# Eight first-layer groups of a block in seven products, and a sum over halves of tokens moved to two DMAs

## The chip, the cores and the metric

The kernel runs on one core of a Trainium2 chip. The metric is the device time of one execution in microseconds (us); lower is better. The core has engines that run side by side, each through its own list of instructions in order: TensorE (PE) multiplies matrices into PSUM, VectorE (DVE), ScalarE (ACT) and GpSimd (POOL) work elementwise, and SyncE (SP) issues DMAs. DMAs move data on 16 DMA engines; those issued by SP go through a hardware queue (q1 in the profile), those issued by POOL through a software queue (q0).

## The reference

Attention with keys and values projected to 64 rows, then a two-layer network with a hard-swish between the layers, over 8 batches of 1024 tokens:

```python
k_proj = np.einsum('ks,bhsd->bhkd', E, k)
v_proj = np.einsum('ks,bhsd->bhkd', F, v)
scores = scale * np.matmul(q, k_proj.transpose(0, 1, 3, 2))
attn = np.exp(scores - np.max(scores, axis=-1, keepdims=True))
attn = attn / (np.sum(attn, axis=-1, keepdims=True) + 1e-09)
x = np.matmul(attn, v_proj)          # to 8192 tokens of 512
h = x @ w_in                          # 512 to 2048
g = h * np.clip(h + 3.0, 0.0, 6.0) / 6.0
out = g @ w_out                       # 2048 to 512
```

## The kernel before, in words

**Blocks.** Each batch b is two blocks (t = 0 and 1) of 512 tokens. The main loop (line 858) runs over batches 1 to 7; batch 0 is worked ahead of it. In a block PE computes the first layer of this block, `h` in 16 groups of 128 columns, and the second layer of the block behind it. Attention of the next batch (`second`) and the projection of the one after that (`third`) are fitted in at places that a plan names.

**The order is written out.** A string names the steps of a block one by one (`ORDER`, and `QUADS` from batch 3 on), and every engine gets its instructions in that order. `L0` to `L15` are first-layer groups: 8 matmuls of 512 columns into a PSUM tile `mm` (`first_group`, line 581), then `h_out` (573): ACT writes relu(h/6 + 0.5) to `r`, DVE writes min(r, 1) times h to `g`. The PSUM pools hold four tiles `mm` and four tiles `at`.

**The second layer in pairs.** `A`, `B` and `N` steps are the seven products of Strassen's scheme (in Winograd's form) for the second layer; A and B belong to the block behind, N starts on this block. Each is 16 matmuls of 256 columns (`Pair`, 684). They need sums of blocks of `g`, made by class `Sums` (662): `c` adds the first half of tokens of the eight low groups to the second half, into a tile `sc` (on POOL); `a` changes the second half in place to a difference (DVE); `b` and `d` make `sb` (DVE) and `sd` (POOL). Step 5 reads `sc`, step 6 the result of `a`, steps 1 and 3 `sb` and `sd`.

**The first layer in a quad.** From batch 3 on the last four groups of a block (12 to 15) are also made in seven products, steps `Q1` to `Q7` of 8 matmuls of 256 columns each (`Quad`, 746), from four sums of x (`xc`, `xa`, `xb`, `xd`, POOL) and three sums of w_in (`v_sums`, made in batch 1; two blocks of w_in are changed in place in batch 3). ACT copies products 7, 2 and 5 out of PSUM (`copied`, 773), DVE subtracts, and `out` (778) applies the hard-swish: three of four outputs by ACT (relu), POOL (min with 1, line 789) and POOL (product, 790), the fourth by ACT and DVE.

**Delays.** `behind_steps(n)` lets an instruction be recorded n steps later; `later` holds small works that are taken one at a time after certain steps.

**Queues.** SP's queue holds, in this order within a batch, stores of output rows (709), the inverse sums and their spreading (330, 336), and the transposes of keys and queries (251, 188). POOL's queue issues the loads of k, v and q of a later batch (`load_kqv`, 124), each set behind a one-element copy `mark` (218) that waits for the transposed queries. The plan of batch 3 issues such a load at the start of its first block; from then on `third.load_next` issues it at `L7` of a second block.

The order from batch 3 on before the change:

```python
    QUADS = ("L0 A7 L1 A6 L2 B7 L3 A1 L4 B2 L5 A3 L6 B5 L7 A4 "
             "L8 Q7 Q2 B6 L9 Q6 N2 Q5 B1 L10 Q1 B3 L11 Q3 N5 B4 Q4").split()
```

## Time and profile before

| what | value |
|---|---|
| time, median of 3 runs | 478.25 us (477.89 to 478.27) |
| the profiled execution's span | 476.3 us |
| PE / PEld busy | 99% / 73% |
| DVE / ACT / POOL busy | 71% / 58% / 64% |
| DMA packets, bytes moved | 84609, 68.65 MB |
| output stores (SP), median to landing | 4.2 us for 256 KB |
| spread sums (SP), median to landing | 6.1 us for 256 KB |
| loads of k, v, q (POOL), 1 MB each, median to landing | 11.4, 15.9, 21.0 us |
| granted TensorE clock | 1.00 in every window asked for |

The span is the time from the first to the last instruction of the profiled execution; the measured time has about 2 us more around it. In a line of the trace's groups, such as `L790 POOL TENSOR_TENSOR g<-r,qm 128x512 bf16<-128x512 f32 x27 | 36.3, 1345 | 2.3`, the fields are the source line, engine, operation, written and read tiles, shapes, how many, then total busy us and mean ns of one, then the idle time of the engine just ahead of them. In a timeline the first number is the start in us from the span's start and the second the length. Lengths of matmuls overlap, so what a step costs is read from start to start.

### The profile page before, as it was taken

How to read it: one execution, taken by the hardware profiler on the slowest of the kernel's cores; microseconds unless marked ns; L12 is line 12 of the kernel's file. 1: busy time of each engine (PE TensorE's matmuls, PEld its weight loads, DVE VectorE, ACT ScalarE, POOL GpSimd, SP SyncE). 2: the span in 40 equal slices, each digit the busy share in tenths (PEclk: the TensorE clock that was granted, in tenths of full speed). 3: DMA queues.
4: the chain of work that ended last, by engine and by line, in shares of the span. 5: the costliest groups of instructions: out<-in, count | busy, mean ns of one | idle time of the engine just before them, and what ended most of it. 6: DMA issues, size and time to landing. Idle time of an engine off the chain costs nothing.

```text
span 476.3 us, 14916 instructions
## 1 busy us (share of the span) xinstructions
PE 469.6 (99%) x6428; PEld 346.1 (73%) x6428; DVE 339.4 (71%) x542; ACT 275.4 (58%) x534; POOL 306.1 (64%) x207
## 2 busy tenths in 40 slices
PE   7999999999999999999999999999999999999997
PEld 4554567667677766787787878778687877878797
DVE  2583387688765958886778876887778897747574
ACT  3766478675455654656466565666457545546451
POOL 8634966153335232867897778887788587888820
DMA  9999989688999939996999196962931054111012
GB/s 166 198 200 207 240 146 207 124 144 149 238 180 156 214 100 200 200 206 157 192 165 171 48 228 136 211 126 89 205 101 47 36 125 136 45 47 45 33 59 90
DMA packets 84609, 68.65 MB, mean 144 GB/s; under 512 B 38336, under 2 KB 70592, under 8 KB 84544
## 3 DMA queue, kind: packets, MB, share of 16 engines
q0 software_dynamic: 33024, 29.36, 39.7%
q1 hardware_dynamic: 51152, 37.83, 33.1%
q8 instruction: 50, 0.82, 0.7%
q10 hardware_dynamic: 368, 0.52, 0.3%
q14 instruction: 15, 0.12, 0.1%
HBM read 71.83 MB, written 16.97 MB: 186 GB/s over the span
## 4 chain that ended last, share of the span: by engine, by line
PE 92%; DMA 3%; ACT 2%; POOL 1%; DVE 0%; issue 0%; POOLq 0%
PE mm L200 68%; PE at L200 21%; DMA w_in_sb<-in_moe_w_in_dram 2%; PE at L289 2%; DMA k<-in_k_dram 1%; PE at L268 1%; ACT aT L277 1%; POOL k L110 0%; POOL q L106 0%; PE at L459 0%; DVE parts L309 0%; ACT rec L212 0%; ACT rec L206 0%; ACT m L705 0%; PE at L439 0%
## 5 line engine op out<-in xcount | busy, mean ns | idle before, releaser
L200 PE MATMUL mm<-xT,w_in_sb 128*64 128x512 bf16 (+1 forms) x1808 | 221.8, 375 | 0.2
L576 DVE SCALAR_TENSOR_TENSOR g<-r,mm 128x512 bf16<-128x512 f32 x216 | 146.2, 681 | 70.7 <-ACT r L575 69.8
L575 ACT ACTIVATE r<-mm 128x512 f32<-128x512 f32 x216 | 128.3, 598 | 117.3 <-PE mm L200 111.1
L200 PEld LDWEIGHTS <-w_in_sb 128*64 128x64 bf16 x2048 | 117.0, 110 | 59.7 <-issue 3.3
L200 PEld LDWEIGHTS <-g 128*64 128x64 bf16 x2048 | 112.6, 110 | 24.0 <-issue 4.1
L139 POOL TENSOR_TENSOR sd<-g,sb 128x1024 bf16<-128x1024 bf16 x28 | 59.1, 2130 | 42.0 <-DVE sb L139 40.7
L136 POOL TENSOR_TENSOR sc<-g 128x2048 bf16<-128x2048 bf16 x14 | 57.0, 4072 | 44.7 <-DVE g L576 44.7
L200 PE MATMUL mm<-w_out_sb,g 128*64 128x256 bf16 (+1 forms) x1088 | 77.8, 286 | 0.0
L200 PE MATMUL at<-w_sums,g 128*64 128x256 bf16 x896 | 58.4, 273 | 0.3 <-DVE g L576 0.3
L789 POOL TENSOR_SCALAR r<-r 128x512 f32<-128x512 f32 x27 | 41.5, 1538 | 15.2 <-ACT r L784 15.2
L705 ACT COPY m<-at 128x256 f32<-128x256 f32 x84 | 31.4, 373 | 30.1 <-PE at L200 25.6
L790 POOL TENSOR_TENSOR g<-r,qm 128x512 bf16<-128x512 f32 x27 | 36.3, 1345 | 2.3
L301 DVE TENSOR_TENSOR xT<-at,rec 128x512 bf16<-128x512 f32 x54 | 34.9, 683 | 2.3 <-DMA rec<-turned_rows 1.6
L139 DVE TENSOR_TENSOR o_sb<-m,mm 128x256 f32<-128x256 f32 x60 | 24.8, 413 | 9.6 <-PE mm L200 7.3
L200 PE MATMUL mm<-w_out_sb,sd 128*64 128x256 bf16 x480 | 31.3, 273 | 0.0
L200 PE MATMUL mm<-w_sums,sb 128*64 128x256 bf16 x480 | 31.2, 273 | 0.0
L277 ACT ACTIVATE aT<-at 128x512 bf16<-128x512 f32 x52 | 29.6, 601 | 2.3 <-PE at L268 2.3
L309 DVE TRANSPOSE_TENSOR_REDUCE parts<-aT 128x32 f32<-128x1024 bf16 x24 | 29.7, 1236 | 0.3 <-ACT aT L277 0.3
L200 PEld LDWEIGHTS <-sd 128*64 128x64 bf16 x480 | 26.5, 110 | 3.9 <-issue 0.2
L200 PE MATMUL at<-w_out_sb,sc 128*64 128x256 bf16 x448 | 29.3, 273 | 0.0
L200 PEld LDWEIGHTS <-sc 128*64 128x64 bf16 x480 | 26.5, 110 | 3.8 <-issue 0.3
L200 PEld LDWEIGHTS <-sb 128*64 128x64 bf16 x480 | 26.2, 110 | 4.0 <-issue 1.6
(118 smaller groups left out, 496.3 us busy)
## 6 DMA issues: line engine op xcount, KB each, us to landing
out_dram<-o_sb SPq DMA_DIRECT2D x60, 256.0 KB, 4.2
rec<-turned_rows SPq DMA_DIRECT2D x48, 256.0 KB, 6.1
k<-in_k_dram POOLq DMA_DIRECT2D x7, 1024.0 KB, 11.4
v<-in_v_dram POOLq DMA_DIRECT2D x7, 1024.0 KB, 15.9
q<-in_q_dram POOLq DMA_DIRECT2D x7, 1024.0 KB, 21.0
w_in_sb<-in_moe_w_in_dram POOLq DMA_DIRECT2D x7, 256.0 KB, 9.9
w_out_sb<-in_moe_w_out_dram POOLq DMA_DIRECT2D x3, 512.0 KB, 14.2
k<-in_k_dram POOLq DMA_DIRECT2D x4, 256.0 KB, 6.0
```

The costliest lines, as they stand in the source:

```text
L136: engine.tensor_tensor(out=out, in0=x, in1=y, op=ALU.add)
L139: engine.tensor_tensor(out=out, in0=x, in1=y, op=ALU.subtract)
L200: nc.tensor.matmul(ps[lo:lo + width], stationary[:, lo:lo + width], moving, **flags)
L277: when(lambda r=r: nc.scalar.activation(aT[:, :, r, :], tiles[r].rearrange("p (a n) -> p a n", a=2), AF.Exp, scale=scale))
L289: nc.tensor.matmul(tiles[t][c:c + D], stationary(r, 2 * j + a), self.weights(j, a)[r:r + KP], start=True, stop=True)
L301: when(lambda t=t: nc.vector.tensor_mul(self.xT[:, j, t, :], av[t], rec[:, t]))
L309: nc.vector.tensor_reduce(out=self.parts[:, j], op=ALU.add, axis=mybir.AxisListType.X, apply_transpose=True, in_=self.aT[j].rearrange("p a ...
L575: nc.scalar.activation(r, h_ps, AF.Relu, bias=0.5, scale=1.0 / 6.0)
L576: when(lambda: nc.vector.scalar_tensor_tensor(g[:, fo, :], r, 1.0, h_ps, op0=ALU.min, op1=ALU.mult))
L705: self.copy(m, ps)
L789: nc.gpsimd.tensor_scalar(out=r, in0=r, scalar1=1.0, scalar2=None, op0=ALU.min)
L790: nc.gpsimd.tensor_tensor(out=g, in0=r3, in1=h3, op=ALU.mult)
```

## The change

1. From batch 3 on groups 8 to 11 of a block are made like groups 12 to 15: a second quad `R` with its own sums of w_in. Both quads use the same four sums of x, and their copies share the buffers `qm7`, `qm2`, `qm5`. `L8` to `L11` are gone from the order, `R1` to `R7` are added.
2. The clip of the six outputs of a block that POOL multiplies moves to ACT: relu(0.5 - h/6) and then relu(1 - r) in place of relu(0.5 + h/6) on ACT and min on POOL. These outputs are those of both quads; in the last block all go by DVE as before.
3. From batch 3 on `c` is two DMAs: `+c` copies the first half of tokens of the eight low groups into `sc` (SP's queue), `+C` adds the second half to it (POOL's queue; it waits for the copy). `a` of the low groups then waits for `+C`.
4. The orders are new: `b`, `d`, the sums of x, `c` and `a` stand in them as `+` entries, and there are two orders for the last batch. The works of attention stand in tables (`PLANS`) with other places: the load in batch 3 moves from the start of the first block to `L3`, the later loads from `L7` to `Q1` of the second block, and batches 1 and 2 have changed places too. The sums of w_in for both quads are made in batch 1, the in-place changes in batch 3 at `L1` and `L3`.
5. One spare buffer of `aT` goes (five to four), and `ones` is smaller. The rest of the diff is assertions that what a product reads has been written.

```diff
+ORDER_OF_QUADS = ('L0 R7 A7 L1 +b +x L2 L3 L4 +d L5 L6 B2 A6 R2 R6 L7 R5 B7 B5 A1 +c R1 Q7 B6 A3 +C R3 Q6 B1 '
+                  'A4 Q2 B3 N2 Q5 Q1 N5 +a R4 Q3 B4 Q4')
+ORDER_OF_LAST = (('R7 L0 +b +x L1 R2 L2 A7 A6 L3 L4 +d L5 L6 B2 R6 L7 R5 B7 B5 +c A1 Q7 R1 B6 +C A3 R3 Q6 B1 '
+                  'A4 Q2 B3 N2 Q5 Q1 N5 +a R4 Q3 B4 Q4'),
+                 ('L0 R7 +x A7 +b L1 L2 R2 L3 L4 L5 L6 B2 R6 A6 L7 R5 +d A1 B7 B5 Q7 R1 +c B6 A3 R3 Q6 +C B1 '
+                  'A4 Q2 B3 N2 Q5 Q1 N5 +a R4 Q3 B4 Q4'))
+PLANS = {
...
+    3: ('0.L1:S01 0.Q2:u0 0.L5:S23,u1 0.B5:u2 0.A1:u3 0.Q2:T 0.N2:I 0.B4:p 1.Q1:m 1.L3:V01 1.B1:V23 '
+        '0.L3:l 0.L1:iR 0.L3:iQ'),
+    4: ('0.L1:S01 0.Q2:u0 0.L5:S23,u1 0.B5:u2 0.A1:u3 0.Q2:T 0.N2:I 0.B4:p 1.Q1:m 1.L3:V01 1.B1:V23'),
+}
+RELU_BEHIND = 2
+PRODUCT_BEHIND = 3
+L_BEHIND = 1
...
+    quarters = {"Q": Quarter(FO - 2 * NQ), "R": Quarter(FO - 4 * NQ)}
...
         def c(self, engine=nc.gpsimd):
             self.sc = spool.tile([P, KH, HT], bf16, tag="sc", name="sc")
-            add(self.sc, self.blocks[0], self.blocks[2], engine)
...
+            if engine is None:
+                nc.sync.dma_start(out=self.sc, in_=self.blocks[0])
+            else:
+                add(self.sc, self.blocks[0], self.blocks[2], engine)
+
+        def c_added(self):
+            assert not self.ready
+            nc.gpsimd.dma_start(out=self.sc, in_=self.blocks[2], accum_op=ALU.add)
...
-                nc.scalar.activation(r, h, AF.Relu, bias=0.5, scale=1.0 / 6.0)
...
-                    nc.gpsimd.tensor_scalar(out=r, in0=r, scalar1=1.0, scalar2=None, op0=ALU.min)
+                    nc.scalar.activation(r, h, AF.Relu, bias=0.5, scale=-1.0 / 6.0)
+                    nc.scalar.activation(r, r, AF.Relu, bias=1.0, scale=-1.0)
                     nc.gpsimd.tensor_tensor(out=g, in0=r3, in1=h3, op=ALU.mult)
...
-            at((0, "A6"), lambda: add(v12, v12, v22, nc.gpsimd), lambda: sub(v21, v21, v22, nc.gpsimd))
```

In a plan an entry such as `1.Q1:m` reads: in the second block, after step Q1, do m. The letters are: S scores, V values, u the sums of exps, T and I the turning and spreading of these sums, P the projection of the next batch, p that of the batch after it, l the load behind the next batch, m the load behind the batch after it, w the sums of w_in and i the changes in place. At a step named in the `+` entries: b, d, x (sums of x), c, C, a.

## The prediction

> **What bounds the kernel now.** I read the share of each engine first, then TensorE (PE) in order of time in one block of batch 5, then the groups of instructions with their shapes kept apart. From the page:

> ```profile
> PE 469.6 (99%) x6428; PEld 346.1 (73%) x6428; DVE 339.4 (71%) x542; ACT 275.4 (58%) x534; POOL 306.1 (64%) x207
> PE mm L200 68%; PE at L200 21%; DMA w_in_sb<-in_moe_w_in_dram 2%; PE at L289 2%; DMA k<-in_k_dram 1%; PE at L268 1%; ACT aT L277 1%; POOL k L110 0%; POOL q L106 0%; PE at L459 0%; DVE parts L309 0%; ACT rec L212 0%; ACT rec L206 0%; ACT m L705 0%; PE at L439 0%
> ```

> PE is busy for 99% of the span and 89% of the chain that ended last is products of line 200. Every other engine has idle time. The timeline of PE (start, length, work) shows whether "busy" also means "at its pitch":

> ```profile
> 319.02 1.03 PE L200 MATMUL mm<-xT,w_in_sb 128*64 128x512 bf16 x8
> 319.89 0.60 PE L200 MATMUL mm<-xa,w_in_sb 128*64 128x256 bf16 x8
> 320.32 1.04 PE L200 MATMUL at<-w_sums,g 128*64 128x256 bf16 x16
> 321.20 0.60 PE L200 MATMUL at<-xc,w_in_sb 128*64 128x256 bf16 x8
> 321.63 1.04 PE L200 MATMUL mm<-w_sums,sb 128*64 128x256 bf16 x16
> ```

> From start to start: a plain group L (8 matmuls of 512 columns) takes 0.87 us, a step of a pair (16 of 256) 0.87 to 0.88, a step of a quad (8 of 256) 0.43. So 512 columns cost 108 ns, 256 cost 54 ns, and steps follow without a gap. A block of batches 3 to 7 has 12 L, 14 pair steps and 7 quad steps: 26 x 0.867 + 7 x 0.433 = 25.6 us. The last block (436.8 to 462.5) takes 25.7, so PE runs at its pitch there, and only fewer columns, or a stall, can move the time. Projection, scores and values add 4.8 us a batch (55.9 us a batch).

> **The products: minus 4.3 us.** In ten blocks the groups L8 to L11 (32 matmuls of 512 columns, 3.47 us) become seven R steps (7 x 0.433 = 3.03 us): 0.434 us less a block, 4.3 in all. A block is then 25.14 us of PE.

> **The other engines, priced where there is room.** VectorE (DVE): four products of 0.68 us become three subtractions and one product of 0.69; nothing changes. ScalarE (ACT) and GpSimd (POOL):

> ```profile
> L784 ACT ACTIVATE r<-qm 128x512 f32<-128x512 f32 x30 | 19.0, 633 | 9.2 <-DVE qm L139 9.2
> L775 ACT COPY qm<-at 128x512 f32<-128x512 f32 x30 | 16.4, 586 | 0.0
> L789 POOL TENSOR_SCALAR r<-r 128x512 f32<-128x512 f32 x27 | 41.5, 1538 | 15.2 <-ACT r L784 15.2
> L790 POOL TENSOR_TENSOR g<-r,qm 128x512 bf16<-128x512 f32 x27 | 36.3, 1345 | 2.3
> L136 POOL TENSOR_TENSOR sc<-g 128x2048 bf16<-128x2048 bf16 x14 | 57.0, 4072 | 44.7 <-DVE g L576 44.7
> ```

> ACT gains three copies of 0.586 and six clips of 0.633 a block, 5.6 us; it was busy for about 17.5 us of a first block (t=0) and 16 of a second, so it comes to 23.1 of 27.6 and 21.6 of 26.2. POOL loses the sum (4.07) and three clips (1.54 each), gains three products (1.345) and one DMA issue (0.9): minus 3.7. Both are hidden behind PE; if ACT's cover were gone, the 5.6 us would show (a rival below). The new plans of batches 1 and 2 and the new orders can recover at most the few tenths that PE stands still there: I take minus 0.3, bounds minus 1 and plus 2 (six weight sums of 1.16 us now stand together on POOL, ahead of the d sums of 4.2 us).

> **The sum of halves: where it goes.** It leaves POOL for a copy on SP's queue, a wait, and an adding DMA on POOL's queue. No row shows either, so I bound them.

> ```profile
> q0 software_dynamic: 33024, 29.36, 39.7%
> q1 hardware_dynamic: 51152, 37.83, 33.1%
> q<-in_q_dram POOLq DMA_DIRECT2D x7, 1024.0 KB, 21.0
> DMA to landing us min/median/max: 2.0/2.0/2.7
> DMA to landing us min/median/max: 2.0/5.8/8.3
> DMA to landing us min/median/max: 21.2/21.2/21.2
> ```

> (The last three: output stores from 400 to 450 us, with no load running; stores from 295 to 320, beside a load of the next batch; the q load of 295.5.) A packet of q1 takes 0.331 x 16 x 476.3 / 51152 = 49 ns for 740 bytes, one of q0 92 ns for 889. Each DMA here has 1024 pieces of 512 bytes, 64 to an engine. By bytes that is 34 ns x 64 = 2.2 us at q1's rate and 53 ns x 64 = 3.4 us at q0's; by packets of q0 it is 5.9 us, the upper end. The copy is q1's kind: 2.2 us. The add reads SBUF like the copy, but reads twice and goes through q0: I take the middle of the two rates, 2.8 us, and keep 2.2 and 5.9 for the range. Around the data the packet records show 0.83 us from issue to first packet on SP and 1.7 on POOL (0.9 of it the issue), and 0.3 from last packet to semaphore. So copy 3.3 us, add 4.8 us. A DMA cannot take less than its data, so no end is below nothing.

> [...]

> **When the add can start.** Times from a block's first matmul. In an unloaded second block (batches 3 to 6) V01 has added 0.55 us: step R1 ends at 14.85. Its subtraction on DVE (0.69) is done at 15.6; ACT first copies Q7 (ends 15.3) until 15.9, then clips R1 twice (0.63 each) until 17.1; POOL's product of R1 (1.35) stands ahead of the add and ends at 18.4. The copy is queued on SP behind the store of A1 (ended 14.4, subtraction 0.4, issue 0.33): out at about 15.2, landed at 18.5. So the add is issued at 18.4 and lands at 23.2. Who needs it: step N5, at 22.1 + 1.1 (values) = 23.2. No stall, no slack. Behind the waiting add on POOL stand the products of R3 and Q6; ACT's copy of Q2 waits for R3's (they share a buffer), and step Q5 for that copy: 0.3 us of room. On DVE the difference a of the low groups now waits for the add, and behind it the last products; what needs these is L2 of the next block, 3 us later.

> Batch 6, t=0: scores add 0.95, R1 ends later, add issued at 18.8, lands 23.6, N5 at 23.05: 0.55. Batch 7: nothing inserted, N5 at 22.1, add issued at 18.2, lands 23.0: 0.9 in each of two blocks.

> **Beside a load.** The load of a batch's k, v, q (three of 1 MB) occupies q0 for 21 us. In batches 3 and 4 it now starts at Q1 of the second block, behind the add and two products on POOL: first issue at 23.2, q out 1.8 later, landed 21.2 after that, so 20.0 us into the next first block (batches 4 and 5). There the copy, out at 15.4, shares the engines (stores took 5.8 instead of 2.0 us) and lands at about 20.5; the add lands at 25.3 against N5 at 23.05: 2.25 us, twice.

> Batch 3, t=0, is the worst. Before, the load was issued as the block began:

> ```profile
> 189.00 0.18 POOL L218 COPY mark<-qT 1x1 bf16<-1x1 bf16 x1 [8.82 <-DMA qT<-q]
> 189.23 0.93 POOL L124 DMA_DIRECT2D k<-in_k_dram  x1
> 189.94 1.28 DVE L301 TENSOR_TENSOR xT<-at,rec 128x512 bf16<-128x512 f32 x2
> ```

> Now it stands on POOL behind two in-place weight sums and the four sums of x, and xa needs the last xT (done at 191.2): three sums of 1.2 us, mark, k issued at 195.0, q at 196.8, landed at 218.0, that is 28.7 us into a block that began at 189.35. Loads on q0 land one behind the other (k 11, v 16, q 21 us), so the add's packets come after q's: 31.5 at the earliest. N5 stands at 23.05: 8.45 us.

> **The sum.** 8.45 + 2 x 2.25 + 0.55 + 2 x 0.9 = 15.3 of stalls, less 4.3 and 0.3: plus 10.7. The execution's span of 476.3 with 1.95 around it is the median of the runs, 478.25; so 489. With the add's data at 2.2 us the stalls are 11.8 (485.4); at 5.9 they are 11.55 + 2 x 5.35 + 3.65 + 4 x 3.1 + 2 x 4.0 = 46.3 (520).

> **Rivals.** (1) Everything lands in time: the fast side. Place: N5 of every block; decides from an add that lands by 23 us in every block, batch 3 too, which needs the add's packets to pass the load's, or the load to be through by 19. For it: PE loses nothing else, and in most blocks I find 0 to 0.9 us short, within the error of my chain. Against: landing order of k, v, q. Time: 478.25 - 4.6 = 473.6. (2) The add is slow (q0's price by packets, or by elements): each block pays 2 to 5 us; 495 to 520. For it: packets on q0 are nearly twice as dear as on q1. (3) ACT becomes the bound in first blocks, where exps come on top: 84% busy in order, 1 us in each of five blocks, DMAs in time but for batch 3: 478.25 - 4.6 + 8.45 + 5 = 487; alone without batch 3's stall 478.7.

> **Chances.** A difference under 0.2% cannot be told from none. Forecast (batch 3 pays, others little; 480 to 494): 0.45. Everything in time: 0.27. Slow add: 0.19. ACT, and mixtures around no change: 0.09. Faster 0.28, same 0.04, slower 0.68. The forecast's own range is 481 to 494. The whole range runs from 473 (rival 1) to 505 (half of rival 2).

> **What would show it.** Batch 3, t=0: PE idle about 8 us ahead of the products that read sc, released by a DMA on q0, landing after that load's q. Batches 4 and 5, t=0: some 2 us there; other blocks under 1. R steps at 0.43 us. Wrong if the wait for sc is under 1 us in batch 3, if the add's packets cost over 60 ns, or if PE waits mostly for r or qm from ACT.

## The result: 551 us, 15% slower, and the profile after

| | before | after |
|---|---|---|
| time, median | 478.10 us (4 runs) | 550.98 us (4 runs) |
| ratio, 95% interval | | 1.152 (1.150 to 1.155) |
| span of the profiled execution | 476.3 us | 548.3 us |
| mean granted TensorE clock | 1.00 | 0.947 |

The forecast, 489 (473 to 505), had the sign and the place of the loss right and its size far too small; it had the late landing, but no term for the clock. One execution each of e7, e9b and e14 (below) fell into a slow state, of 806 to 1236 us, and is left out of their ratios. The chain that ended last, before:

```profile
PE 92%; DMA 3%; ACT 2%; POOL 1%; DVE 0%; issue 0%; POOLq 0%
```

Five lines from the page of after: busy times, the granted clock in 40 slices, the chain that ended last, and the two new DMAs with their median from issue to landing.

```profile
PE 491.1 (90%) x6668; PEld 369.8 (67%) x6668; DVE 346.9 (63%) x545; ACT 319.7 (58%) x618; POOL 286.8 (52%) x212
...
PEclk9999999999999998599897998989989799798989
...
PE 61%; DMA 24%; POOL 4%; DVE 3%; ACT 3%; issue 3%; SPq 0%; POOLq 0%; DVEq 0%; ACTq 0%
...
sc<-g SPq DMA_DIRECT2D x10, 512.0 KB, 3.6
sc<-g POOLq DMA_DIRECT2D x10, 512.0 KB, 7.6
```

PE falls from 99% to 90% busy, the DMAs' share of the chain rises from 3% to 24%, the copy lands as forecast (3.6 us against 3.3) and the add does not (7.6 against 4.8). From the 16th slice on, within batch 3, the clock is no longer full. What PE waited for (total us, times, longest):

```profile
PEld L251 <- DMA sc<-g: 31.7, 10, 4.2
...
ACT qm L855 <- POOL g L877: 24.0, 10, 10.7
PE at L251 <- ACT qm L855: 19.9, 9, 10.5
```

Ten blocks, ten waits for the add. The other two lines are one chain: ACT may copy quad product 2 only when POOL has multiplied out of that buffer; POOL's product stands behind the add, which waits for the copy; PE's step Q5 waits for ACT. One block, from the timelines of POOL and then of PE (start, length, work):

```profile
455.96 1.27 POOL L877 TENSOR_TENSOR g<-r,qm 128x512 bf16<-128x512 f32 x1 [2.35 <-ACT r L876]
458.20 1.58 POOL L736 DMA_DIRECT2D sc<-g  x1 [0.97 <-PE at L340]
```

```profile
462.19 0.63 PE L251 MATMUL mm<-xb,v_sums 128*64 128x256 bf16 x8
466.01 1.92 PE L251 MATMUL at<-w_out_sb,sc 128*64 128x256 bf16 x16 [3.19 <-DMA sc<-g]
467.72 1.06 PE L251 MATMUL mm<-xT,w_in_sb 128*64 128x256 bf16 x8
468.57 1.06 PE L251 MATMUL mm<-xd,w_in_sb 128*64 128x256 bf16 x8
469.42 1.92 PE L251 MATMUL mm<-w_out_sb,g 128*64 128x256 bf16 x16
```

N5 was due at 462.62, when the quad step before it was through. The add was issued at 458.20; with the forecast's 4.8 us it lands at 463.0, 0.4 us late; it landed at 466.0. (The view puts the 0.97 us ahead of the add down to PE; the add waits for the copy, which had landed at 457.64.) Then N5 takes 1.71 us from start to start where a pair step takes 0.87, and the steps behind it 0.85 where 0.43 is a quad step's. The granted clock by stretches of this block (PE busy, PEld, DVE, ACT, POOL busy, clock, DMA share, GB/s) says why:

```profile
462.00:466.00 4.00, 0.82 (x16) 0.55 (x11) 0.73 (x3) 0.58 (x1) 0.32 (x1) 0.86 0.89 142
466.00:469.00 3.00, 2.99 (x30) 2.52 (x31) 0.68 (x1) 1.00 (x3) 0.00 (x0) 0.50 0.00 0
469.00:472.00 3.00, 3.00 (x34) 2.58 (x32) 1.29 (x2) 1.63 (x4) 1.27 (x1) 0.55 0.00 0
472.00:478.00 6.00, 6.00 (x84) 4.34 (x80) 4.54 (x6) 4.30 (x9) 4.94 (x3) 1.00 0.12 46
```

The clock is half from 464.9, still within the wait, to 471.7: some 6 us of work, then it is full. In the 3.41 us up to 464.89 PE was busy for 1.06, or 31%: the clock fell though PE was not idle throughout (last section).

**The balance.** The waits ahead of Q5 and N5 in the ten blocks sum to about 53 us: 14.5 in batch 3, t=0, and 3.6 to 4.7 in each of the others. PE's busy time at a clock below full, times the part of the clock that is missing, summed over half-microsecond windows, is 21.5 us in ten stretches, one in each block; before it was nil. The saved columns are -4.3. That makes +70.2 of the span's +72.0; the rest is small waits.

### The profile page after: what moved, and what is told of

Its sections match the earlier page's. It is cut to its first block, busy times and chain, and to the rows that moved or that the text cites. A ratio compares the mean times of both kernels' runs of the same rounds, so it can differ in the third digit from the quotient of the medians.

```text
span 548.3 us, 15542 instructions
## 1 busy us (share of the span) xinstructions
PE 491.1 (90%) x6668; PEld 369.8 (67%) x6668; DVE 346.9 (63%) x545; ACT 319.7 (58%) x618; POOL 286.8 (52%) x212
## 4 chain that ended last, share of the span: by engine, by line
PE 61%; DMA 24%; POOL 4%; DVE 3%; ACT 3%; issue 3%; SPq 0%; POOLq 0%; DVEq 0%; ACTq 0%
PE mm L251 42%; DMA sc<-g 20%; PE at L251 17%; DMA w_in_sb<-in_moe_w_in_dram 2%; DVE g L628 1%; DMA kT<-kp 1%; DMA k<-in_k_dram 1%; ACT aT L328 1%; PE at L319 1%; DVE xT L353 1%; POOL g L877 1%; PE at L340 1%; ACT r L625 1%; POOL sd L176 1%; POOL k L147 0%
## 5 line engine op out<-in xcount | busy, mean ns | idle before, releaser
L251 PE MATMUL mm<-xT,w_in_sb 128*64 128x512 bf16 (+1 forms) x1568 | 184.9, 377 | 1.4 <-DVE g L628 1.3
L628 DVE SCALAR_TENSOR_TENSOR g<-r,mm 128x512 bf16<-128x512 f32 x176 | 117.2, 680 | 47.3 <-ACT r L625 46.8
L625 ACT ACTIVATE r<-mm 128x512 f32<-128x512 f32 x176 | 103.8, 600 | 66.0 <-PE mm L251 61.7
L877 POOL TENSOR_TENSOR g<-r,qm 128x512 bf16<-128x512 f32 x54 | 74.0, 1483 | 113.4 <-ACT r L876 113.4
L855 ACT COPY qm<-at 128x512 f32<-128x512 f32 x60 | 35.0, 583 | 36.7 <-POOL g L877 24.0
L251 PEld LDWEIGHTS <-sc 128*64 128x64 bf16 x480 | 28.7, 123 | 34.7 <-DMA sc<-g 31.7
L176 DVE TENSOR_TENSOR qm<-qm,mm 128x512 f32<-128x512 f32 x40 | 27.0, 675 | 25.0 <-PE mm L251 15.2
L875 ACT ACTIVATE r<-qm 128x512 f32<-128x512 f32 x54 | 33.9, 628 | 11.1 <-DVE qm L176 11.1
L876 ACT ACTIVATE r<-r 128x512 f32<-128x512 f32 x54 | 34.0, 630 | 1.7
L176 DVE TENSOR_TENSOR g<-g 128x1024 bf16<-128x1024 bf16 (+3 forms) x29 | 22.5, 776 | 15.8 <-DMA sc<-g 15.6
L176 DVE TENSOR_TENSOR qm<-mm,qm 128x512 f32<-128x512 f32 x20 | 13.8, 691 | 28.4 <-PE mm L251 27.7
## 6 DMA issues: line engine op xcount, KB each, us to landing
k<-in_k_dram POOLq DMA_DIRECT2D x7, 1024.0 KB, 10.4
v<-in_v_dram POOLq DMA_DIRECT2D x7, 1024.0 KB, 15.8
q<-in_q_dram POOLq DMA_DIRECT2D x7, 1024.0 KB, 20.8
```

The source lines that it names most:

```text
L176: engine.tensor_tensor(out=out, in0=x, in1=y, op=ALU.subtract)
L251: nc.tensor.matmul(ps[lo:lo + width], stationary[:, lo:lo + width], moving, **flags)
L625: nc.scalar.activation(r, h_ps, AF.Relu, bias=0.5, scale=1.0 / 6.0)
L628: nc.vector.scalar_tensor_tensor(g[:, fo, :], r, 1.0, h_ps, op0=ALU.min, op1=ALU.mult)
L855: nc.scalar.copy(m, ps)
L875: nc.scalar.activation(r, h, AF.Relu, bias=0.5, scale=-1.0 / 6.0)
```

## The experiments

Theories: (T1) the pair of DMAs costs nearly all of it, by landing late; (T2) much of it is the new work of ACT, POOL and DVE, or the place of the steps. Each edit below is against the changed kernel, unless another is named. The versions that keep the pair of DMAs (e3 to e6, e10 to e13 and e15) were run once each; the four runs of the changed kernel lie 2.5 us apart, so a difference of that size between two of these versions says nothing.

**The sum back on an engine (e1, e2).** All else stays changed.

```diff
-"c": lambda: sums.c(None), "C": sums.c_added
+"c": lambda: sums.c(), "C": lambda: None            # e1, GpSimd
+"c": lambda: sums.c(nc.vector), "C": lambda: None   # e2, VectorE
```

> The sum of halves is made by POOL again, where the copy stood (+c); nothing stands at +C. All else is the changed kernel. Theory 1 (the pair of DMAs lands late, TensorE idles before N5 in each block and then runs at half clock for some us): the loss goes whole, 474 us (478.25 less 4.3). Theory 2 (the second quad and ACT's clips cost it: shared buffers, ACT too full): at most the DMA waits of 29 us go, so 510 to 525.

> The sum of halves is made by DVE (about 1.2 us each, by the one such sum of batch 0) where the copy stood; nothing at +C. Theory 1: 474 us, with no wait for sc and a granted clock of 1.00. Theory 2: 510 to 525, as for the sum on POOL.

e1: 483.98, ratio to before 1.011 (1.007 to 1.015); e2: 486.98, 1.018 (1.015 to 1.021). The clock is full in both. So the pair of DMAs, with the clock it costs, is worth 67 us of 73. But even without it the change is 6.0 us slower than before instead of 4.6 faster: some 10 us that neither theory had. On DVE the sum costs 3 us more, because R1's subtraction stands behind it and step R3 waits for that. In e1's trace step Q3 waits in the first block of batches 3 to 6 for Q1's subtraction, which stands on DVE behind the reciprocal sums (I); two steps at the start of the next block wait for work that ACT and DVE do late because the projection's casts (p) stand there.

**The reciprocal and the projection moved (e7, e8), on top of e1.** e7 moves only I, e8 also p.

```diff
-0.N2:I 0.B4:p
+0.Q1:I 1.L6:p
```

> The kernel with the sum on POOL (e1, 484), and the inverse of the sums of exps at Q1 in place of N2, so that DVE does Q1's subtraction before the reciprocal (0.93 us). If DVE's order is what holds Q3 back (1.0 us in each first block), 480 to 481. If ACT is (its copies of Q2 and Q5 come late), no change, 484.

> As e7, and the projection of the batch after next at L6 of the second block in place of B4 of the first, so that its four copies (2.3 us of ACT) no longer stand among the outputs of the quads. If ACT's backlog there is what holds back L5 and A7 of the second block (1.3 us a batch), 475 to 476; if it comes from elsewhere (sb and a on DVE), as e7.

e7: 481.30, 1.0064 (1.0047 to 1.0080), what its theory had, to 0.3 us. e8: 479.68, 1.0034 (1.0021 to 1.0046): 1.6 of the 5 us or more that were expected. Four waits of 0.71 us ahead of Q4, one in each of batches 3 to 6, are left, again for a subtraction on DVE.

**The last waits (e9, e9b, e14), on top of e8.** e9 moves the difference `a` on DVE behind that subtraction; e9b also moves I to B4; e14 is e9 with two buffers for the copy of product 2.

```diff
-N5 +a R4 Q3 B4 Q4
+N5 R4 Q3 B4 +a Q4
```

> Edit: as e8 (sum on GpSimd, reciprocal I right behind Q1, projection p at L6 of the next block), and the difference a of the low groups on VectorE moves from ahead of R4 to behind B4, in all three orders. Before: 478.2. Theory (what is left of e8's loss is the 0.71 us per batch that step Q4 waits for Q3's subtraction, and a, 0.62 us on VectorE, stands directly ahead of that subtraction): four waits of 0.71 shrink to about 0.1 to 0.2, so 479.7 - 4 x 0.55 = 477.5 (477 to 478.3). Rival (VectorE is short of time there whatever the order, the wait moves to Q4's own products or to the next block): 479.2 to 480.5.

> Edit: as e9, and the reciprocal I moves once more, from behind Q1 to behind B4. Theory (the run of I, 5 us on VectorE, is what makes Q3's subtraction late; moved behind the last pair steps nothing waits for it before the projection at L6): the 0.71 per batch and the 0.45 in batch 3 go, 476.0 to 477.2, below the kernel before by the columns saved. Rival (I then stands ahead of the products of the block's end and of the next block's first groups, which wait for it; or the projection waits): 479 to 482.

> Edit: as e9 (479.1, sum on GpSimd), and the copy of the second quad difference in two bf16 buffers. What is left in e9 against the kernel before: 1.04 us ahead of Q5 and 0.45 ahead of R3 in batch 3, 0.76 in the last block, some 3 us of waits under 0.4 us. Theory (the 1.04 is the one buffer, freed late by GpSimd, which has batch 3's weight and x sums first): 478.0 (477.6 to 478.4), no change against before. Rival (as in e4 the wait moves on): 479.

e9: 479.07, 1.0017 (1.0004 to 1.0029), next to the rival's range; the four waits of 0.71 are gone, but only 0.6 of their 2.8 us came back. e9b: 482.49 (1.0085, 1.0070 to 1.0100), past the rival's bound; where it waits was not seen. e14: 477.98, ratio 0.9994 (0.9985 to 1.0003): no difference from before. Its time is the theory's, but not by the theory's way alone: in batch 3 the wait moved from Q5 to Q3 (1.34 us). So even with the sum on GpSimd and four places mended, what the R steps save in columns (4.3 us) goes into new waits of PE: this one, 0.76 us in the last block, and many under half a microsecond.

**The load in batch 3 (e3).** It is issued when the block starts, not at L3.

```diff
-0.L3:l
+0.start:l
```

> The changed kernel with the load of batch 3 at the start of its first block, as before the change, in place of L3. If the add waits there behind the load's packets (theory 1), the 14.5 us of stall before Q5 and N5 in that block shrink to the 4 to 6 us of the other blocks, and with them some half-clock time: 538 to 543. If the wait there has another cause (the copy itself, slowed by any traffic), 549 to 552.

546.16, in between. The waits ahead of Q5 and N5 in batch 3 fell from 14.5 to 7.0 us, and a new one of 2.4 appeared behind the scores: 5.1 net, 4.8 measured. In the changed kernel the packets of the load's three transfers end at 217.6 us; the copy, issued at 205.0 beside them, took 12.9 us instead of 3.6, and the add was out only then. In e3 the load still lands only at 212.3, and the copy, issued at 207.7, takes 7.0 us. So the place of the load was a cause, for about 5 us, and much of what batch 3 still waits above the other blocks' 3.6 to 4.7 us comes from the load too. The new wait is not for the load's data. With its issues out of the way earlier, GpSimd makes its sums beside DVE's sum `sb`, which then takes 4.5 us, and PE waits for a product on DVE behind it (first the changed kernel, then e3):

```profile
193.60 1.26 DVE L176 TENSOR_TENSOR sb<-g 128x2048 bf16<-128x2048 bf16 x1
...
194.06 4.51 DVE L176 TENSOR_TENSOR sb<-g 128x2048 bf16<-128x2048 bf16 x1
```

**The clock (e5).** Sixteen unread matmuls stand ahead of each N5, about 34 us of work in all (some 3.4 us in the block around 457 us of e5's trace).

```diff
+                        for _ in range(16):
+                            nc.tensor.matmul(idle, w_in_sb[:, 0, :P], xT[:, 0, t, :], start=True, stop=True)
```

> The changed kernel with 16 products of 512 columns (3.4 us of TensorE) that nobody reads ahead of each N5 from batch 3 on: 34 us of added work. If idling is what halves the clock afterwards, the added work fills the wait, the clock stays at 1.00 and the time falls in spite of it, to 525 to 540. If the clock falls for another reason (the adding DMA, or power), the time stays at 551 or rises, to 585 at most.

539.62: 11 us faster with 34 us more work. The clock rose from 0.947 to 0.987, and the busy time lost at half clock fell from 21.5 to 3.0 us, all of that in batch 3. So idling at N5 cost its wait and then 2 us a block of slow work (21.5 us in ten blocks).

**The shared buffer (e4).** The copy of product 2 gets two buffers in bf16.

```diff
-m = spool.tile([P, TOK], f32, ...)
+m = spool.tile([P, TOK], bf16 if name == "m2" else f32, ..., bufs=2 if name == "m2" else 1)
```

> The changed kernel with two buffers for the copy of product 2 (both in bf16, which rounds that one product more coarsely), so that Q2's copy no longer waits for R3's product on POOL, which stands behind the adding DMA; Q5 then need not wait. If the add's landing is what ends last in each block, N5 waits longer by what Q5 waited less: 548 to 552. If the shared buffer was a loss of its own, the 19.7 us of waits ahead of Q5 go: 531 to 536.

551.34. Q5 no longer waits; N5 waits 15.9 us in batch 3 and 3.6 to 4.9 elsewhere. The chain by way of ACT that the wait list shows is real, but not the bound: behind it stands the landing.

**The pair earlier (e6).** A1 and B5 stand right behind L7, `+c` behind B5, `+C` ahead of R1, and N5 behind B4, about 3 us of slack at each end.

```diff
-L7 R5 B7 B5 A1 +c R1 Q7 B6 A3 +C R3 ... Q5 Q1 N5 +a R4 Q3 B4 Q4
+L7 A1 B5 +c R5 B7 +C R1 Q7 B6 A3 R3 ... Q5 Q1 +a R4 Q3 B4 N5 Q4
```

> The changed kernel with the same DMAs at other places: A1 and B5 right behind L7, the copy behind B5, the add two steps on and ahead of R1's product on POOL, N5 two steps later, behind B4. If it is only the place (the add lands 11 us after the copy is issued, whatever stands around it), the waits for sc go in all blocks but the first of batch 3, and the clock stays at 1.00 there: 490 to 500. If the DMAs cost in themselves (slower loads and stores, engines kept from SBUF), 515 or more.

513.97, between the two expectations and nearer to the second: the place is worth 37 us, 18 of it by the clock (3.0 us lost at half clock). The landing no longer holds N5; the products queued behind the waiting add hold Q5, and step Q3 waits 0.8 to 2.1 us in nearly every block.

**How much of the pair can be hidden (e10, e11).** e10 is e6 with the two buffers; e11 has the early load and the moved I and p too.

> Edit: as e6 (the copying and adding DMA keep the sum, but start some 3 us earlier and N5 stands behind B4), and the copy of the second quad difference gets two buffers in bf16. e6 took 514. Theory (e6's remaining Q5 waits, 22 us in all, come from the one buffer, which GpSimd frees late because the product of R3 stands behind the waiting add; N5 now has slack): the waits outside batch 3, about 11 us, go; batch 3's 11 us move to N5, since the add still lands behind the load: 500 to 505. Rival (as in e4 the wait only moves, to N5 or to the steps whose products stand behind the add on GpSimd): 509 to 515.

> Edit: as e10, with batch 3's load issued as the block starts (e3), the reciprocal I behind Q1 and the projection p at L6 of the next block (e8). It asks how much of the pair of DMAs can be hidden at all. Theory (what is left in e10 is the load in batch 3, worth some 8 to 11 us with the clock, and VectorE's backlog at Q3, 0.8 to 2.1 us a batch, 9 us in all): 485 to 493, still above the 479.7 of the same kernel with the sum on GpSimd. Rival (GpSimd's queue behind the waiting add is the cost, whatever lands when): over 497.

518.27 and 519.00: neither is better than e6. e11 is its rival's case, e10 lies past its rival's range. Two lines of e10's waits show that PE waits most for a subtraction on DVE (step Q3 for that of Q1), and that DVE waits for the add:

```profile
PE mm L251 <- DVE qm L176: 24.0, 13, 9.3
...
DVE g L176 <- DMA sc<-g: 15.1, 7, 3.8
```

What DVE did meanwhile, in a first block of e11, and what POOL did:

```profile
279.34 0.31 DVE L370 STREAM_TRANSPOSE turned<-parts 128x128 f32<-128x128 f32 x1
279.68 4.05 DVE L373 COPY turned<-turned 32x128 f32<-32x128 f32 x1
283.77 0.28 DVE L374 TENSOR_TENSOR inv<-turned 32x128 f32<-32x128 f32 x1
284.06 0.22 DVE L373 COPY turned<-turned 32x128 f32<-32x128 f32 x1
...
284.97 0.68 DVE L176 TENSOR_TENSOR qm<-qm,mm 128x512 f32<-128x512 f32 x1
```

```profile
279.41 4.23 POOL L877 TENSOR_TENSOR g<-r,qm 128x512 bf16<-128x512 f32 x3
```

The same copy takes 4.05 us and then 0.22. The long one ends when POOL's three products do, and those ran together because they had queued behind the add. Q1's subtraction (284.97) stands behind it, and step Q3 waits for it until 285.65, 3.9 us. (The expectations below call this step R3.)

**The held copy, and the difference that waits (e12, e13, e15), on top of e11.** e12 takes out the copy and the addition of the turned halves (the second half of the sums is left out); e13 also moves `+a` behind N5; e15 keeps the sum and writes the copy as a maximum of the tile with itself.

```diff
-nc.vector.tensor_copy(other[here], turned[there])
-nc.vector.tensor_add(inv[...], turned[here], other[here])
+nc.vector.transpose(inv[...], turned[here])                                   # e12, e13
+nc.vector.tensor_tensor(out=other[here], in0=turned[there], in1=turned[there], op=ALU.max)  # e15
```

> Edit: as e11 (519), but the two copies and two additions on VectorE that add the turned halves of the softmax sums are replaced by two transposing moves of the first half; this leaves out the second half of those sums. Theory (the copy is held until GpSimd's run of products ends, 4.05 us in e11 against 0.22 us alone, and Q3's subtraction, queued behind it, makes step R3 wait 3.9 us in the first blocks of batches 4 to 6 and in batch 3): four waits of 3.9 shrink to under 1.5, and with them the half clock behind each (7.5 us in all): 500 to 508. Rival (the subtraction waits for something else, the copy merely fills the time): 515 to 520.

> Edit: as e12, and the difference a of the low groups moves on VectorE from ahead of R4 to behind N5. It waits there for the add's landing (14.4 us in eight waits in e11) with Q3's subtraction queued behind it. Theory (that queue is the rest of R3's waits): 3 to 8 us below e12, and R3's waits under 0.3 us; N5's own waits of 0.7 to 1.3 us stay. Rival (a costs nothing there): within 1.5 us of e12.

> Edit: as e11 (519), but the copy of the turned half is written as the maximum of the tile with itself, an instruction with two inputs, instead of a copy. Theory 1 (any VectorE instruction that reads SBUF twice is held by a GpSimd product, as the sums sb of 1.2 us are that take 2.1 beside GpSimd in e1): still 2 to 4 us for it, 514 to 520. Theory 2 (only the copy form is held; the additions of the same tiles took 0.28 us in e11, though GpSimd was through by then): 0.28 us, and the time falls as in e12, 500 to 508.

e12: 518.57. Locally the theory held: Q3's waits of 3.9 us in the first blocks of batches 4 to 6 fell to 0.8 to 1.0. But the time did not move: N5 now waited 1.6 to 2.9 us in those blocks, and `a` took the copy's place on DVE ahead of the next subtraction:

```profile
284.92 0.69 DVE L176 TENSOR_TENSOR g<-g 128x1024 bf16<-128x1024 bf16 x1 [2.10 <-DMA sc<-g]
285.53 0.68 DVE L176 TENSOR_TENSOR qm<-mm,qm 128x512 bf16<-128x512 f32 x1
```

e13, with `a` out of the way: 505.86, 12.7 us less, more than the 3 to 8 expected. e15: 519.13; the maximum took up to 5.17 us, so the form of the copy is not what is held. So one holder hides the next. In the best of these versions with the DMAs, e13, 27 us above e9 stay, though half of those sums are left out: N5 still waits 14.5 us for the add in eight blocks, step Q3 10.9 us in ten, PE 2.6 us early in batch 3 behind a held sum `sb` (4.9 us, as in e3), and 3.4 us go at half clock.

## Why the prediction was right in kind and wrong in size

**Right.** The R steps saved their 4.3 us (e8 and e9 have 5.3 to 5.4 us more waits than before and a span only 1.0 to 1.2 longer). The copy: 3.6 us against 3.3, though in part by luck: its packets took 25 ns where 34 had been taken, and the first of them came 1.3 us after the issue where 0.83 had. In four of the ten blocks the add was out within 0.3 us of the forecast: in both of batch 7 (18.4 and 18.3 us into the block) and in the two first blocks of batches 4 and 5 (20.7 and 20.5). The worst block is batch 3, t=0, and it is the load, as said. PE waited at N5 for `sc`.

**Right by luck, or late.** "Beside a load" had the copy slowed by a load in the first blocks of batches 4 and 5. It was not: it took 3.5 and 3.6 us, since the load had landed before the copy was issued, some 14 us into the block instead of 20.0. The copy was issued 1 us later than forecast, and so the add's time came out by luck. In the second blocks of batches 3 to 6 the copy was out 0.8 to 1.6 us late. The add followed the copy's landing by 0.6 to 0.7 us (as in nine of the ten blocks) and was out at 20.1 to 22.6 us instead of 18.4.

**Mis-sized: the add. This step failed first.** "I take the middle of the two rates, 2.8 us ... So copy 3.3 us, add 4.8 us." It took 7.6. Its issue held POOL 1.58 us where the loads' 0.9 had been taken, and its packets of 512 bytes took 71 ns each in the median (64 to an engine, 4.5 us) where 44 ns had; over 60 ns was one of the prediction's own signs of being wrong. That lay within the bounds kept (2.2 to 5.9 for the data). It was the middle of two rows of transfers that do not add. The add's packets cost 2.8 times the copy's (71 ns against 25). "No stall, no slack" then made each of the 2.8 us missed a stall in ten blocks: 28 us.

**Mis-sized: batch 3.** 14.5 us instead of 8.45. The forecast had the add's packets behind the load's. In the trace the copy, on its own queue, was stretched to 12.9 us beside the load as well, and the add could be issued only then.

**Missing: what a wait does to the clock.** The sum had 108 ns for 512 columns behind every stall. At half clock the quad steps took 0.85 us where 0.43 is theirs at full clock, so 213 ns for 512 columns, for 3.4 or 6.8 us in each block (17.1 in batch 3, t=0); 21.5 us in all. With the add at 7.6 us the prediction's own steps give 4 x 2.8 + 2 x 5.05 + 3.35 + 2 x 3.7 + 10.2 = 42 us of stalls (10.2 in batch 3, t=0, where only the add's data come behind the load's), 516 us; with the 53 us measured and the clock it is 548. The 11 us between 42 and 53 are batch 3 and, in the main, the late adds of the second blocks.

**Wrong: "Both are hidden behind PE".** ACT's new clips and copies, and the moved works of attention, were set at nothing, with 1 us in each of five blocks as a rival. e1 shows some 10 us in their place, and by moving DVE's reciprocal and the projection e8 gets 4.3 of them back. Utilisation (84% of ACT) said too little; which instruction stands ahead of which said more.

**The rivals.** "The add is slow" was the nearest, and its 520 was the upper end worked out; it had a chance of 0.19 and the range was cut at half of it.

## What to carry to other kernels

A transfer that must land "with no slack" should be forecast as late: price it at the dear end, for each block, and add what the wait does to the clock (here 21.5 us in ten blocks). When work moves from an engine to a DMA that other engines wait for, list what is queued behind each waiting instruction (here POOL's products behind the add, DVE's subtraction behind `a`); with the DMAs started earlier, these queues still held PE in every block. Where PE had to wait some 3 us in each block, unread matmuls ahead of N5 were cheaper than idling (e5: 11 us less for 34 us of added work); no other kernel was tried.

## What the runs showed of the hardware that was not expected

```profile
461.48:464.89 3.41, 1.06 (x16) 0.79 (x15) 1.24 (x2) 1.08 (x3) 0.84 (x1) 1.00 1.21 188
464.89:468.31 3.42, 2.30 (x22) 1.96 (x24) 0.69 (x1) 0.34 (x2) 0.00 (x0) 0.50 0.02 3
...
308.33:311.74 3.41, 1.19 (x24) 1.02 (x20) 1.16 (x2) 0.90 (x3) 3.41 (x4) 1.00 0.83 95
311.74:315.16 3.42, 3.42 (x36) 3.36 (x34) 2.10 (x3) 2.46 (x6) 3.42 (x6) 0.50 0.72 74
...
400.49:403.90 3.41, 1.61 (x26) 1.23 (x23) 2.10 (x3) 2.60 (x6) 2.98 (x3) 1.00 1.19 180
403.90:407.32 3.42, 1.86 (x30) 1.66 (x32) 1.41 (x2) 1.20 (x3) 2.77 (x3) 1.00 0.05 6
```

- The VectorE copy with a median of 0.22 us took up to 4.05 us (e11), and written as a maximum with two inputs, with a median of 0.29 us, up to 5.17 (e15). In the traces of the two kernels seven of the 24 copies took 1.4 us or more (1.44 four times before; 2.57, 3.04 and 3.98 after), and each of them ended 0.1 us after a GpSimd sum or run of products that was under way. In e11, above, the copy ended at 283.73 and the run of three products at 283.64; in e15, in the same place, the maximum of 4.09 us ended at 283.63 and the run at 283.48. So there it was held until the last of three GpSimd products in a row had ended; by what was not shown.
